# A fused attention and gated-MLP kernel: another order of all its steps, with two weight pieces decoded first and warm-up products on TensorE

## The chip, the cores and the metric

The kernel runs on one core of a Trainium2 chip. A core has four compute engines that the text calls PE (TensorE: matmuls, with PEld for its weight loads), DVE (VectorE), ACT (ScalarE) and POOL (GpSimd), and SP (SyncE), which here only issues DMA transfers. Each engine runs its own instructions strictly in order and waits at each for what it needs; sixteen DMA engines carry what SP issues. The metric is the device time of one execution in microseconds, as the median of several runs. One further execution was profiled, and all durations of single instructions come from it.

## The reference

For 4 batches, 8 heads, 768 tokens and head width 64, each chunk of 32 queries attends to 8 memory keys and to a window of keys from 16 before to 8 after the chunk. The result, as 768 tokens by 512 columns, goes through a gated MLP with a spatial product.

```python
for c in range(nc):                      # chunks of 32 tokens
    k_full = concat([mem_k, k[l_start:r_end]]); v_full = concat([mem_v, v[l_start:r_end]])
    scores = scale * q_c @ k_full.T
    a = exp(scores - max(scores)); a = a / (sum(a) + 1e-9)
    out[c] = a @ v_full
x = out                                   # (4, 768, 512)
h = gelu_tanh(x @ w_in)                   # (4, 768, 1024)
u, v = h[..., :512], h[..., 512:]
v_n = (v - mean(v)) / sqrt(var(v) + 1e-6) * g_ln
v_s = einsum('ts,bsd->btd', w_sg, v_n) + b_sg[None, :, None]
return x + (u * v_s) @ w_out
```

In this case the weights w_in and w_out arrive as 64-bit floating point numbers, seen by the kernel as two 32-bit words for each, so they must be decoded on the chip before they can be used.

## The kernel before

The work is cut into 24 attention units, one for each batch and each block of 128 tokens (unit u is batch u // 6, block u % 6), and into MLP products. Everything is written as named steps, and the string ORDER says in which order they are issued: each name is looked up and its instructions are appended to the program of its engine. Since every engine works in order, ORDER fixes the sequence on each engine, including SP's queue of transfers; across engines only data dependencies and the reuse of buffers hold work back. A star behind a name takes the step's second engine. Nothing else orders the work.

The steps, with the engine (second engine after a slash):

- `q`, `k`, `v` + u (SP): the transfers of a unit's queries (256 KB), keys (368 KB) and values (512 KB). There are two buffers for q and k and three for v, so q2 and k2 wait until unit 0's scores are done.
- `S` u (PE): scores; `mx` (DVE) row maxima; `sb` (DVE) subtraction, which also empties the single score buffer in PSUM, so that S of the next unit waits for it; `ex` (ACT) exponent; `z` (POOL) zeroes missing keys in the first and last block; `sm`, `sr` (DVE) sum and reciprocal; `nm` (DVE / POOL) normalising. `T` (PE) transposes the result and `p` (ACT / DVE) copies it to SBUF for units below 10; later units use `yt` (DVE) and the transfers `Ea` to `Ed`.
- `A` u (PE): the product with the values; `xc`, `xh` (ACT), `xl` (POOL / DVE, or DVE alone for units 0, 2, 4, 5): the result in 32 bits, and split into a high and a low part for the products that follow.
- `ri` + half + piece (SP): one of eight pieces of w_in, 512 KB each; half 1 is for v, half 0 for u. `d1` (ACT / POOL), `d2` (DVE / ACT), `d3`, `d4` (DVE), `d5` (ACT), `d6` (POOL / DVE) decode it into a high and a low part. Pieces i10 and i11 make up the first half of the columns for v, i12 and i13 the second. `ro` and `d..o` are the same for w_out; `g`, `ga`, `gb` load and split w_sg; `cb` and `cbh` the small vectors.
- `V` bt (PE): h for v, 12 products of 512 columns for a block of 128 tokens; `v1` to `v4` its gelu, `v5`, `vx`, `vy`, `v6` its statistics, `v7` normalising, `v8`, `v9` the split. `Va` and `Vb` are the two halves of V in 12 products of 256 columns each; blocks listed in VSPLIT are made that way.
- `U` bhj (PE): h for u, 12 products of 384 columns, `u1` to `u4` its gelu; `W` bhj (PE): the spatial product, 18 products; `w1` to `w4` gate it; `O` bhj (PE): the output product, 12 products; `o1` (DVE) adds x; `out` (SP) stores.
- `zz` + n: n warm-up products of the identity with itself, written into the PSUM buffer that is free next and read by nobody. Each is one 128-column product and appears in the trace as two matmul instructions.

T, V, U, W and O share four PSUM buffers, handed out in turn. Every operation is recorded through one helper, so the profile gives nearly all of them the line L106; they are told apart by their tiles: `s` scores, `e` exponents, `n` normalised, `av` the product with the values, `pt` its transposed factor, `raw`, `ex`, `m` the stages of decoding, `w_in_hi` and `w_in_lo` the decoded weights, `mm` the shared PSUM buffers, `pair` the split input.

```python
    def warm(n):
        for _ in range(n if mms.free else 0):
            tensor.matmul(mms.free[0][:, 0:P], ident, ident, start=True, stop=True)

    for name in ORDER.split():
        if name[0] == "z" and name[1] == "z":
            warm(int(name[2:]))
            continue
        does, eng = steps.pop(name.rstrip("*"))
        does(eng[name.endswith("*")])
```

Of the kernel before, what the change touches and what calls it, by code (L numbers as in the profile page):

```python
# [55 lines left out]
w4000 d6o2 w4002 w1012 S13 mx13 z12 sm12 w2012 A9 z11 sm11 w1011 w2011 w3012 sr11 nm11 yt11 O000 O003 sb13
o1003 O001 u2013 u3013 sr12 o1001 v12 k15 v10 S14 O002 mx14 W013 nm12 ex13 w3011 xh6 xh8 w4012 sb14 u4013 xh7
xl8 V12 w1013 w2013 v112 w3013 o1002 o1000 ex14 w4013* Ed5 Ea5 k16 q15 Ec5 q16 Eb5 out003 S15 out001 out002
out000 k17 w4011* xl7 sm14 v212 yt12 sr14 sm13 V11 v312 sr13 v111 v211 v311 w4010 xl6 O011 U101 nm13* mx15
v411 sb15 v412 v512 yt13 vx12 xc9 A10 u1101 xc10 S16 vy12 v612 v511 A11 ex15 sm15 o1011 vx11 vy11 v611 v711*  # L60
nm14* v712 v812 v912* V10 mx16 U103 v110 v210 v310 u1103 U102 sr15 u2101 v410 sb16 ex16 sm16 u3101 sr16 u4101
v510 u1102 O012 v811 vx10 o1012 q17 S17 mx17 k18 q18 Ea6 Ec6 Eb6 Ed6 out011 O013 O010 u2102 xc11 u3102 xh9
v911 vy10 v610 yt14 o1013 nm15 sb17 u2103 xl9* A12 S18 V13 yt15 v710* v810 xh10 xh11 u4102 xl11 o1010 u3103
v113 xl10 v213 v313 v413 v14 out012 v13 out010 out013 k19 q19 q20 k20 V15 U110 u1110 v513 vx13 u4103 v910 mx18
nm16 sb18 vy13 v613 v713* U113 V14 xc12 v115 v215 v315 u2110 v813 ex17 u1113 v913 A13 S19 v114 v415 v515 vx15
u2113 u3113 v214 v314 v414 v514 vx14 u4113 vy15 z17 v615 v715* U100 U112 U111 u1100 v815 ex18 vy14 v614 v714
u3110 v814 u4110 u1111 v914* u2100 u2111 u3111 u4111 v915 W111 w1111 w2111 sm17 Ed7 W103 w1103 w2103 mx19 W101
w1101 sr17 w3111 w4111 xc13 w3103 u3100 v15 Eb7 Ec7 v16 Ea7 yt16 nm17* W100 A14 w2101 sb19 S20 w3101 u1112
xc14 u2112 u3112 ex19 u4100 w1100 w2100 A15 W102 W110 w1102 w2102 W113 w1110 w1113 w3100 w3102 w2110 w2113
yt17 w4103 W112 w4100 w4102 z18 w4101 w1112 w3110 w3113 O100 w4110* O103 sm18 sr18 u4112 w2112 w3112 o1103  # L70
# [575 lines left out]
```

## Time and profile before

| | |
|---|---|
| median of 3 runs | 385.7 us (384.4 to 385.95) |
| profiled execution, its own time | 383.29 us |
| span of the profiled execution | 381.5 us |
| PE busy | 363.9 us, 95% of the span |
| DVE busy | 247.5 us, 65% |
| ACT busy | 155.3 us, 41% |
| POOL busy | 131.3 us, 34% |

The busy share is an average over stages that differ: the span begins with a stretch in which weights arrive and are decoded while the first units run, and goes on with a long stretch of MLP products. Time lost is read from the stretch where PE waits, by what ended its wait. The time of an execution is a little longer than the span from its first to its last instruction.

### The profile page before, as it was taken

The page shows a single profiled execution, that of the slowest core. Times are in us where ns is not written, and L with a number is a line of the kernel's source. Part 1 is how long each engine was busy: PE and PEld are TensorE (multiplying, and loading weights), DVE is VectorE, ACT ScalarE, POOL GpSimd, SP SyncE. Part 2 cuts the span into 40 slices and gives each one's busy share as a digit, 9 for nine tenths or more (in the row PEclk, how much of TensorE's full clock was granted, in tenths as well). Part 3 has the DMA queues.
Part 4 walks back from the last instruction along what each step waited for, and adds up shares of the span by engine and source line. Part 5 has one row for each costly group of instructions (what it writes and reads, how often), then busy time and mean ns, then how long its engine had stood idle before and what let it go on. Part 6 is the DMA issues. An engine that isn't in the chain of part 4 may idle for free.

```text
span 381.5 us, 11092 instructions
## 1 busy us (share of the span) xinstructions
PE 363.9 (95%) x4788; PEld 340.7 (89%) x4788; DVE 247.5 (65%) x460; ACT 155.3 (41%) x296; POOL 131.3 (34%) x152
## 2 busy tenths in 40 slices
...
GB/s 242 350 316 308 309 181 212 225 66 171 207 173 163 159 74 211 130 95 74 4 11 140 117 217 14 144 10 140 25 3 54 189 50 2 3 0 2 0 63 147
DMA packets 24530, 47.66 MB, mean 125 GB/s; under 512 B 4384, under 2 KB 13600, under 8 KB 24480
## 3 DMA queue, kind: packets, MB, share of 16 engines
...
HBM read 36.96 MB, written 6.29 MB: 113 GB/s over the span
## 4 chain that ended last, share of the span: by engine, by line
PE 94%; DMA 3%; issue 1%; DVE 1%; SPq 0%; POOL 0%; POOLq 0%
PE mmd L106 23%; PE mmc L106 22%; PE mmb L106 19%; PE mma L106 17%; PE av L106 7%; PE s L106 5%; DMA qb<-in_qs 2%; DMA ka<-in_ks 1%; SPq L106 0%; POOL na L106 0%; DVE ea L106 0%; DVE mxa L106 0%; DVE xb L106 0%; POOLq L106 0%
## 5 line engine op out<-in xcount | busy, mean ns | idle before, releaser
L106 PE MATMUL s<-ka,qa 64*32 64x64 f32 x768 | 11.0, 238 | 6.2 <-DMA ka<-in_ks 4.2
L106 PEld LDWEIGHTS s<-ka,qa 64*32 64x32 f32 x768 | 8.9, 112 | 7.9 <-issue 5.1
L106 DVE SCALAR_TENSOR_TENSOR mmc<-mmc,g_half,b_half 128x384 f32<-128x384 f32 x10 | 6.2, 623 | 12.4 <-PE mmc L106 12.4
L106 DVE SCALAR_TENSOR_TENSOR mmd<-mmd,g_half,b_half 128x384 f32<-128x384 f32 x12 | 7.4, 620 | 10.2 <-PE mmd L106 10.2
L106 DVE SCALAR_TENSOR_TENSOR gb<-gb,mmb 128x512 f32<-128x512 f32 x10 | 6.9, 686 | 9.3 <-ACT gb L106 9.3
L106 PE MATMUL s<-kb,qb 64*32 64x64 f32 x768 | 11.0, 238 | 1.7 <-DVE ea L106 1.5
L106 ACT ACTIVATE ea<-ea 128x512 f32<-128x512 f32 x12 | 7.6, 635 | 11.0 <-DVE ea L106 11.0
L106 DVE STREAM_TRANSPOSE y<-na 128x512 f32<-128x512 f32 x14 | 9.8, 702 | 3.4 <-POOL na L106 1.7
L106 PEld LDWEIGHTS s<-kb,qb 64*32 64x32 f32 x768 | 8.9, 112 | 3.5 <-DVE ea L106 1.8
L106 PEld LDWEIGHTS av<-pt,va 64*64 64x64 f32 x512 | 9.3, 145 | 2.9 <-ACT pt L106 1.7
L106 PE MATMUL av<-pt,va 64*64 64x32 f32 x512 | 10.2, 230 | 1.3 <-ACT pt L106 1.3
L106 PE MATMUL mmc<-w_in_hi,paira 128*128 128x512 f32 (+1 forms) x40 | 9.5, 359 | 1.8 <-issue 1.8
L106 DVE TENSOR_REDUCE mxa<-s 128x8 f32<-128x512 f32 x8 | 5.4, 679 | 8.5 <-PE s L106 8.5
L106 PEld LDWEIGHTS av<-pt,vb 64*64 64x64 f32 x512 | 9.2, 145 | 1.9 <-issue 1.1
L106 POOL TENSOR_TENSOR na<-eb,rda 128x512 f32<-128x512 f32 x3 | 3.5, 1169 | 20.2 <-DVE rda L106 16.4
L106 DVE SCALAR_TENSOR_TENSOR ga<-ga,mmb 128x512 f32<-128x512 f32 x6 | 4.1, 681 | 9.8 <-ACT ga L106 9.8
L106 POOL TENSOR_TENSOR pairb<-uf,pairb 128x384 fp32r<-128x384 f32 x3 | 3.0, 1016 | 20.9 <-ACT pairb L106 20.9
L106 PE MATMUL av<-pt,vb 64*64 64x32 f32 x512 | 10.2, 230 | 0.0
L106 DVE SCALAR_TENSOR_TENSOR mmb<-mmb,g_half,b_half 128x384 f32<-128x384 f32 x6 | 3.7, 617 | 9.9 <-PE mmb L106 9.9
L106 POOL TENSOR_TENSOR paira<-uc,paira 128x384 fp32r<-128x384 f32 x3 | 3.1, 1047 | 20.1 <-ACT paira L106 20.1
L106 ACT ACTIVATE ga<-ga 128x512 f32<-128x512 f32 x12 | 7.6, 632 | 6.0 <-DVE ga L106 5.9
L106 PEld LDWEIGHTS av<-pt,vc 64*64 64x64 f32 x512 | 8.4, 135 | 1.8 <-issue 1.3
...
## 6 DMA issues: line engine op xcount, KB each, us to landing
ka<-in_ks SPq DMA_DIRECT2D x12, 368.0 KB, 4.3
kb<-in_ks SPq DMA_DIRECT2D x12, 368.0 KB, 4.6
va<-in_vs SPq DMA_DIRECT2D x8, 512.0 KB, 5.4
vb<-in_vs SPq DMA_DIRECT2D x8, 512.0 KB, 4.8
vc<-in_vs SPq DMA_DIRECT2D x8, 512.0 KB, 4.6
pt<-y SPq DMA_DIRECT2D x112, 32.0 KB, 1.9
...
```

Of the source, the lines that this page charges most:

```text
L106: return self.tc.keep_in_program_order(getattr(self.engine, name)(*args, **kw))
```

## The change

The diff changes three things. VSPLIT shrinks to (0,), so V of blocks 1 and 2 of batch 0 is made in one piece. In `mm_part` the first half always takes a buffer. And ORDER is another string for all steps. Counted in the strings, the warm-up products go from 4 to 41: seventeen ahead of S0, seventeen between S0 and T0, five ahead of A2, and single ones ahead of A1 and V02. SP's queue now begins with ri11, ri10, k0, q0, ri13, ri12, q1, k1, v0, q2, k2, ri01, k3, q3, v1, ri00, k4, v2, q5, cb, q4, and the d steps of i11 and i10 stand ahead of mx0. PE's sequence begins: 17 products, S0, 17 products, T0, S1, A0, S2, Va00, Vb00, S3, T1, A1, T2, 5 products, A2, S4, T3, V01, S5, A3, V02, T4, S6, V03, U002, S7, A4, U001, U003, V04, T5, S8, A5, T6, U000, V05. Before it was: 3 products, S0, S1, S2, T0, A0, S3, T1, T2, A1, Va00, A2, Vb00, Va01, S4, Vb01, T3, Va02, A3, S5, Vb02, a product, S6, V03, U001, T4, U002, A4, S7, U003, V04, T5, S8, A5, T6, U000, V05. Beside the products, the set of steps is the same but for the halves of V01 and V02.

```diff
@@ -30,68 +30,68 @@
 DIRECT = (0, 2, 4, 5)
 N_U = 7
 ACTX = ()
-VSPLIT = (0,1,2,)
+VSPLIT = (0,)
 
 
 ORDER = """
-zz1 q1 q0 k0 k1 ri11 ri10 zz2 S0 mx0 sb0 ex0 z0 sm0 sr0 q2 k2 S1 mx1 sb1 S2 d2i11* d2i10* ex1 d3i11 d3i10 sm1
-d1i10 d4i10 sr1 v0 ri13 k3 q3 ri12 v1 nm0* d5i10 T0 p0 nm1* A0 mx2 sb2 ex2 sm2 d1i11 d2i13* d1i13 d4i11 d3i13
-sr2 d4i13 d6i10 S3 T1 nm2* T2 xh0 d5i11 xl0 d6i11 xc0 d5i13 p1* A1 d2i12* d1i12 mx3 sb3 d3i12 d6i13* d4i12 xc1
-ex3 sm3 p2 xh1 xl1* v2 d5i12 d6i12* q5 ri00 d2i00* d1i00 ri01 Va00 A2 Vb00 d2i01* d1i01 d3i00 d4i00 d3i01 sr3
-d4i01 d5i00 v100 xh2 v200 v300 q4 ri02 k4 xl2 cb ri03 v3 k5 Va01 S4 q6 k6 g21 g41 g20 g40 g11 nm3* Vb01 T3
-d5i01 d2i02* xc2 v101 p3 d2i03* d1i02 Va02 v400 v500 mx4 vx00 d3i02 cbh v201 sb4 vy00 v600 v700 v800 v900
-d3i03 d4i02 A3 S5 Vb02 mx5 sb5 zz1 S6 ex4 xc3 xh3 sm4 xl3 V03 v301 v401 sr4 v501 d1i03 v102 v202 d4i03 d5i03
-d5i02 v302 ex5 d6i00* nm4 d6i02* d6i01 q7 g10 v6 v4 k7 v5 U001 T4 vx01 vy01 z5 v601 d6i03* ga40 gb40 v402 mx6
-sm5 v701 sb6 u1001 ga11 p4 ga21 ga10 U002 v801 A4 S7 U003 v502 u1002 sr5 u2002 vx02 u2001 ex6 xh4 u3001 xl4
-v901* xc4 v103 u3002 ga41 gb21 gb11 nm5* vy02 z6 v602 gb10 v702* u4001 mx7 sm6 sb7 V04 g51 k8 q8 u4002 v203
-ex7 ga51 v303 T5 p5 sr6 nm6* v403 v503 S8 A5 T6 U000 ga20 v802 mx8 gb51 gb41 gb20 k9 ro0 g30 g01 ga01 xh5 v7
-q10 q9 g31 v902* vx03 gb01 p6 xl5 v104 u1003 xc5 vy03 v603 sb8 v204 u2003 sm7 sr7 u1000 u2000 nm7 V05 ex8
-u3003 ga31 v304 u4003 v703 v404 v803 S9 sm8 v504 vx04 sr8 mx9 v903 A6 T7 xc6 p7 v105 ga30 v205 u3000 g50 q11
-k10 v8 k11 ga50 v305 sb9 u4000 vy04 gb31 gb30 v405 v505 gb50* vx05 nm8* v604 U012 U011 g00 S10 k12 A7 u1012
-u2012 u3012 vy05 v605 mx10 v705 v704 T8 ex9 xc7 p8 U010 U013 v804 u4012 v904* v805 ga00 v905* sb10 A8 S11
-d2o0* d3o0 gb00 d1o0 u1010 ro1 sm9 u1011 d4o0 u2011 ex10 xc8 u2010 u3010 u4010 u3011 u4011 d1o1 W003 d2o1 mx11
...
+zz8 ri11 d1i11 d2i11 d3i11 d4i11 zz3 ri10 d2i10* d1i10 d3i10 d4i10 zz1 zz1 zz1 zz3 d5i11 d6i11 k0 q0 S0 zz4
+zz6 zz4 zz3 ri13 ri12 q1 k1 v0 q2 k2 ri01 d1i13 mx0 sb0 ex0 d2i13* z0 sm0 sr0 nm0 d2i12* d1i12 d3i13 d3i12
+d4i13 T0 S1 p0 A0 mx1 sb1 k3 q3 d5i10 d6i10 d5i13 d4i12 xh0 xl0 S2 Va00 d6i13 ex1 d5i12 d6i12 Vb00 mx2 sm1 sb2
+sr1 d2i01* ex2 d1i01 v100 xc0 S3 v1 ri00 k4 v2 d3i01 sm2 d4i01 mx3 sr2 nm1* T1 nm2* sb3 v200 zz1 p1 d2i00* ex3
+A1 T2 q5 cb q4 ri02 k5 v3 ri03 zz5 v300 xc1 p2 xh1 A2 S4 d3i00 sm3 sr3 nm3 v400 v500 xl1 T3 V01 d1i00 mx4 sb4
+vx00 d4i00 xh2 xl2 ex4 sm4 p3 d2i02* xc2 S5 A3 zz1 cbh vy00 v600 d3i02 sr4 v700 mx5 sb5 V02 nm4* k6 v5 q6 g10
+q7 g40 g11 v4 k7 g20 g21 g30 v101 d1i02 v800 d4i02 xc3 d2i03* d3i03 d5i00 d1i03 xh3 v201 d6i00* ex5 v301 xl3*
+d4i03 d5i02 v900* d5i01 d5i03 v102 T4 S6 d6i02* d6i03 v401 v501 v202 vx01 mx6 sb6 V03 U002 d6i01 z5 vy01 v601
+v701 ga10 p4 ga21 ga20 gb10* gb20* v801 u1002 v302 ga11 v901 gb21 gb11 S7 A4 sm5 sr5 v402 u2002 xh4 xl4 v502
+vx02 g50 k8 U001 ex6 u3002 u4002 z6 v103 u1001 ga40 u2001 v203 mx7 sm6 U003 V04 xc4 ga30 ga50 v303 v403 nm5*
+vy02 gb40 v602 sb7 sr6 q9 q8 g01 v6 k9 g41 ro0 v702 T5 S8 u3001 p5 A5 v802 ex7 u1003 ga41 nm6* u4001 v503 vx03
+mx8 T6 xh5 v902 vy03 v603 gb30 sb8 sm7 p6 v104 sr7 xl5 ex8 v204 sm8 v304 v703 v404 U000 u1000 xc5 nm7* v803
+v903 u2000 u2003 v504 vx04 V05 T7 S9 A6 p7 u3000 u4000 v105 v205 v305 xc6 d2o0* u3003 ga01 mx9 gb50 vy04 v604
+gb41* sr8 v704 sb9 nm8* v804 gb01* v904 v405 u4003 v505 q10 v8 k10 v7 k11 q11 g51 g00 U012 U011 A7 S10 ga51
+u1011 d1o0 d3o0 d4o0 mx10 u2011 vx05 T8 p8 vy05 v605 U013 U010 ga00 sb10 gb00* xc7 u3011 u4011 v705 v805 d5o0
+ex10 u1012 ex9 S11 A8 ro1 gb51* v905* W002 g31 q13 d2o1 u2012 u3012 d3o1 d1o1* d4o1 u4012 xc8 ga31 k12 ro2
...
@@ -482,7 +482,7 @@
 
         def mm_part(eng, h):
             hl = x_pair(b, tt // 3)
-            ps = mms.held[key] if key in mms.held else mms.take(key)
+            ps = mms.held[key] if h else mms.take(key)
             product(eng, ps[:, 256 * h:256 * h + 256], [
                 (lambda a, kt=kt: hl[:, a, kt, sl], lambda c, kt=kt: w_in_hl[c][:, 2 + h, kt])
                 for kt in range(4)
```

## Rows read from the trace of the kernel before

**Rows 1.** The page's first part: the span, and each engine's busy time with its share and its instructions.

```profile
span 381.5 us, 11092 instructions
...
PE 363.9 (95%) x4788; PEld 340.7 (89%) x4788; DVE 247.5 (65%) x460; ACT 155.3 (41%) x296; POOL 131.3 (34%) x152
```

**Rows 2.** Busy time by stretch: the stretch and its length, then for PE, PEld, DVE, ACT and POOL the busy us with the number of instructions, then the granted clock, the share of the DMA engines and what they moved in GB/s.

```profile
12.00:25.00 13.00, 9.09 (x268) 7.52 (x268) 11.99 (x21) 7.91 (x14) 5.54 (x5) 1.00 0.92 336
25.00:42.00 17.00, 15.17 (x346) 14.25 (x342) 14.92 (x27) 14.29 (x26) 8.88 (x8) 1.00 0.92 314
46.00:62.50 16.50, 16.50 (x329) 15.12 (x329) 13.73 (x27) 12.69 (x27) 14.04 (x17) 1.00 0.70 244
46.00:377.60 331.60, 331.60 (x3976) 312.47 (x3975) 214.19 (x402) 127.48 (x248) 115.67 (x129) 1.00 0.31 100
```

**Rows 3.** The chain that ended last in order of time: start, duration, what. The products of Va00, Vb00, the gap in Vb02, a warm-up product (two instructions), V03, T4, A4, S7, V05, O311, and the last addition.

```profile
25.27 2.86 PE mmd L106 x12
...
29.26 1.61 PE mmd L106 x12
...
39.51 1.83 issue
...
41.97 0.22 PE mmb L106 x2
...
42.98 3.00 PE mmb L106 x12
...
48.08 0.44 PE mma L106 x4
...
50.60 1.06 PE av L106 x64
51.66 0.79 PE s L106 x53
...
62.50 2.82 PE mmc L106 x12
...
375.55 2.10 PE mmb L106 x12
377.67 0.56 DVE xb L106
```

**Rows 4.** PE in order of time: start, duration, tile and shape, and in brackets the idle time before it and what ended that. The first warm-up products, S0, T1, T2, A1 and A2.

```profile
1.42 1.65 PE L106 MATMUL mma<-ident 128*128 128x128 f32 x6 [1.42 <-POOL mhalf L106]
7.28 1.17 PE L106 MATMUL s<-ka,qa 64*32 64x64 f32 x64 [4.21 <-DMA ka<-in_ks]
...
19.84 1.11 PE L106 MATMUL mmb<-ident,na 128*128 128x128 f32 x4
22.29 1.12 PE L106 MATMUL mmc<-ident,na 128*128 128x128 f32 x4 [1.33 <-POOL na L106]
23.33 1.93 PE L106 MATMUL av<-pt,vb 64*64 64x32 f32 x64
...
28.05 1.20 PE L106 MATMUL av<-pt,vc 64*64 64x32 f32 x64
```

**Rows 5.** DVE in order of time, same columns: mx0, sb0, sm0, sr0, d3 of i11 and of i10, and xl5.

```profile
8.49 0.69 DVE L106 TENSOR_REDUCE mxa<-s 128x8 f32<-128x512 f32 x1 [8.49 <-PE s L106]
9.21 0.69 DVE L106 TENSOR_TENSOR ea<-s,mxa 128x512 f32<-128x512 f32 x1
10.85 0.69 DVE L106 TENSOR_REDUCE rda<-ea 128x8 f32<-128x520 f32 x1 [0.95 <-POOL ea L106]
11.58 0.20 DVE L106 RECIPROCAL rda<-rda 128x8 f32<-128x8 f32 x1
...
12.98 0.68 DVE L106 SCALAR_TENSOR_TENSOR exb<-rawb,exb 128x512 int32<-128x512 int32 x1
13.58 0.69 DVE L106 SCALAR_TENSOR_TENSOR exa<-rawa,exa 128x512 int32<-128x512 int32 x1
...
61.46 0.69 DVE L106 TENSOR_TENSOR pairb<-av,pairb 128x512 fp32r<-128x512 f32 x1 [0.75 <-ACT pairb L106]
```

**Rows 6.** ACT and POOL in order of time, same columns: ex0, two steps of decoding back to back on ACT; on POOL z0, nm0 and a lower part of decoded weights.

```profile
9.94 0.63 ACT L106 ACTIVATE ea<-ea 128x512 f32<-128x512 f32 x1 [7.93 <-DVE ea L106]
...
10.62 0.20 POOL L106 MEMSET ea<- 32x128 f32 x1 [9.21 <-ACT ea L106]
...
11.94 1.04 POOL L106 TENSOR_TENSOR na<-ea,rda 128x512 f32<-128x512 f32 x1 [1.12 <-DVE rda L106]
...
22.19 1.28 POOL L106 TENSOR_TENSOR w_in_lo<-mb,w_in_hi 128x512 fp32r<-128x512 f32 x1
...
29.00 0.68 ACT L106 ACTIVATE exf<-rawf 128x512 int32<-128x512 uint32 x1
...
29.56 0.69 ACT L106 ACTIVATE mf<-rawf 128x512 f32<-128x512 f32 x1
```

**Rows 7.** Transfers: what had moved in the first 7.2 and the first 8.1 us, and single issues with size and us from issue to landing: k3 (issued at 11.17) and v1 (12.71).

```profile
DMA packets 688, 1.71 MB, mean 238 GB/s; under 512 B 72, under 2 KB 72, under 8 KB 688
...
DMA packets 783, 2.08 MB, mean 256 GB/s; under 512 B 76, under 2 KB 76, under 8 KB 783
...
kb<-in_ks SPq DMA_DIRECT2D x1, 368.0 KB, 6.8
...
vb<-in_vs SPq DMA_DIRECT2D x1, 512.0 KB, 8.4
```

More of the change, by code (lines that the diff above doesn't have):

```diff
@@ L56 @@
[L56 to L70, printed above, removed]
@@ new lines @@
+W001 mx11 w1002 w2002 sm9 sr9 nm9* gb31* d2o2* d6o0* w1001 w2001 w3001 u1010 d1o2 sb11 d3o2 u2010 u3010 W003
+w1003 w2003 W000 u4010 d4o2 T9 w1000 d5o2 ex11 v9 q12 ro3 S12 k13 q14 d6o2 w4001 sm10 p9* w2000 d1o3 w3003
+d5o1 w3000 W010 sr10 w1010 w2010 mx12 w4003 u1013 w3010 w3002 W012 W011 w4000* d6o1 z11 sm11 nm10 d2o3* d3o3
+d4o3 d5o3 sb12 ex12 z12 yt10 d6o3* w4002* S13 mx13 sr11 nm11* w4010 w1012 sm12 w2012 A9 O003 O002 o1003 u2013
+sb13 w1011 w2011 sr12 yt11 O000 O001 xh8 xl8 o1000 o1001 xh6 k14 v10 q15 k15 v11 S14 W013 u3013 mx14 u4013 xh7
@@ new lines @@
+ex13 o1002 w1013 w2013 sm13 xl6 nm12* sb14 V12 w3012 xl7* w4012 Ec5 out003 Ea5 q16 Ed5 out001 k16 out002 S15
+Eb5 out000 v12 U101 V11 v112 v212 w3013 sr13 ex14 w3011 u1101 u2101 w4011* w4013 O011 xc9 A10 v111 v312 yt12
+mx15 nm13 v211 sb15 v412 yt13 sm14 v512 xc10 vx12 S16 u3101 v311 A11 xc11 vy12 v612 v712 v812 ex15 V10 v411
+mx16 o1011 v511 sr14 v912 v110 vx11 v210 v310 v410 v510 u4101 nm14* sb16 vx10 sm15 vy11 v611 v711* U102 v811
+v911* vy10 O010 O012 O013 sr15 o1012 o1013 xh10 xl10* k17 q17 Eb6 Ec6 Ed6 Ea6 U103 A12 S17 xh9 xh11 u1102 xl11
@@ new lines @@
+v610 xl9* yt14 o1010 V13 ex16 u1103 sm16 nm15* mx17 sr16 u2102 sb17 ex17 u3102 u2103 yt15 v710* v810 u4102
+v113 v213 u3103 v313 v413 v910 z17 nm16* v13 out013 out012 v15 k18 k19 q18 out010 v14 out011 q19 V15 v115 v215
+v513 vx13 v315 xc12 v415 v515 u4103 vy13 v613 v713 v813 v913 vx15 U110 u1110 u2110 sm17 V14 U113 S18 U100 v114
+v214 v314 vy15 v615 mx18 sb18 u3110 u1113 v414 v514 vx14 u2113 A13 S19 u1100 v715* v815 v915 u3113 u2100 u3100
+vy14 v614 u4100 u4110 u4113 v714 U112 u1112 v814 v914* sr17 U111 W103 u2112 w1103 w2103 W113 W101 Eb7 k20 Ec7
@@ new lines @@
+yt18 xl14 o1113 sr19 V21 v420 o1110 v520 xl15 V23 A16 nm19* vx20 vy20 v620 v720 o1111 yt19 v820 v920 v121 xc16
+v221 v321 v421 v521 vx21 S21 A17 U202 V22 xh16 v123 mx21 v223 u1202 vy21 v621 v721 v821 v323 xc17 v921 v423
+v523 u2202 v122 xh17 xl16* vx23 vy23 v623 u3202 v222 u4202 xl17 U201 u1201 u2201 u3201 v322 v422 v522 sm20
+U203 u1203 u2203 vx22 v723 v823 q22 out113 out111 v19 Ed9 out110 Ec9 v18 Eb9 q23 Ea9 k23 sr20 u4201 U200 V24
+sb21 v923* u1200 V25 v124 ex21 vy22 v622 u3203 nm20 v722 v822 v224 v324 u2200 u4203 v424 v922* S22 A18 mx22
@@ new lines @@
+v125 v225 xc18 v325 u3200 sb22 v425 sm21 v525 U210 U211 U212 u1210 v524 sr21 vx24 u4200 u2210 vy24 v624 v724
+vx25 vy25 v625 u3210 v725 u4210 u1212 ex22 v824 v825 U213 v925* A19 S23 mx23 u2212 u3212 u4212 v924 W200 W211
+sm22 sr22 yt20 w1200 nm21* w2200 w3200 u1211 u2211 u3211 sb23 xc19 w1211 u4211 w4200 w2211 u1213 w3211 ex23
+W203 w1203 w2203 yt21 W201 w3203 w4203* W210 w1210 w2210 w1201 w2201 w3201 u2213 u3213 Ed10 v20 Eb10 Ec10 v21
+Ea10 u4213 W202 w1202 w2202 w4201 w3210 z23 nm22 yt22 w3202 w4211 w4202 W213 w1213 W212 w1212 w2212 w3212
@@ new lines @@
+w4210* sm23 A20 O201 o1201 w2213 w3213 w4213* w4212* xc20 O203 o1203 sr23 nm23 yt23 O200 A21 O202 O211 O212
+xh19 xh20 o1202 xl20* o1200 o1212 Eb11 out202 Ea11 v22 out203 out212 Ec11 out200 V32 v132 v232 out201 v23 xl19
+V31 v131 o1211 out211 Ed11 v332 v432 v231 xh18 v331 v431 xl18 O213 O210 U301 xc21 xh21 v532 vx32 vy32 v632
+o1213 v732 xl21* A22 U302 v832 u1301 xc22 xh22 v932* v531 u2301 vx31 vy31 v631 u3301 u1302 u2302 u4301 V30
+v130 v230 v330 U303 A23 xl22* v731* v430 u1303 u2303 v530 o1210 V34 vx30 u3302 u4302 xc23 u3303 v831 v931*
```

39 lines of the change are left out of this document (12 added, 27 removed).

## The prediction

> **What bounds the kernel now.** I began with the page's busy line: PE works 95% of the span [rows 1]. The table by stretch says where the other 5% lies [rows 2]: from 46 to 377.6 us PE is busy in all 331.6 us, at 12 to 25 us in 9.1 of 13, at 25 to 42 in 15.2 of 17. The chain of waits in order of time [rows 3] repeats it: from V03's first product (42.98) piece follows piece without a gap until O311 ends at 377.65, and 3.85 us of addition and store close the span. So what comes before 46 us, the ramp, is the one place where time can be won, and a new wait after it the likeliest way to lose some.
>
> In the ramp two things are slow. First, PE runs at its lower level: the twelve products of Va00 took 2.86 us, the same twelve of Vb00 1.61 [rows 3]; a set of transposes 1.11 us at 19.84, 0.44 at 48.08 [rows 3, 4]. [...] Second, DVE: 12.0 of 13 us at 12 to 25, 14.9 of 17 at 25 to 42, 13.7 of 16.5 at 46 to 62.5 [rows 2]. PE waits for it; after 46 us it has a sixth of its time free.
>
> **The change part by part: how early V03 can end.** V03's last product ends at 45.98 in the kernel before [rows 3]. I walk the new order to the same point. Prices: a DVE operation of 512 columns takes 0.69 us but the next starts 0.60 after it when ready (12.98, 13.58), and 0.72 when it needs the result (8.49, 9.21) [rows 5]; ACT starts one each 0.56 (29.00, 29.56); POOL takes 1.28 for a lower part [rows 6]; PE at the upper level 0.79 for scores, 0.44 for transposes, 1.06 for A, 2.8 for V (3.00 right behind scores), 0.22 for a warm-up product [rows 3]; at the lower level three such products took 1.65, or 0.55 each [rows 4].
>
> *Seventeen products ahead of S0.* From 1.42 us they end at 5.2 if all cost 0.22, at 10.8 if all cost 0.55. I take the middle, 8.0.
>
> *S0's data.* ri11 and ri10 (512 KB each) now precede k0 and q0 (368 and 256 KB): 1.69 MB in that order. Before, 1.71 MB had moved by 7.2 us and 2.08 MB by 8.1 [rows 7], so in strict order S0 could start near 7.2. But k0, third of six transfers then, was there only at 7.28 [rows 4], when 1.71 MB had moved instead of the 0.90 MB up to it: later transfers share the engines. Five more follow at once now, so the end could be near 10. I take 8.4. [...] By strict order S0 would come 1.2 us sooner; the trace's 7.28 stands against counting on it.
>
> *Two pieces decoded in DVE's idle time.* Five DVE operations (d2 to d4 of i11, d3 and d4 of i10, 5 × 0.60 = 3.0 us) move to before mx0; until 8.49 DVE had nothing to do [rows 5]. If ri10 lands only near 7 they end near 8.5, before S0 does. That is the gain's source on DVE. ACT's d1, d2 and d5 hide the same way; if this cover were gone, 3.0 us of DVE would be back on the ramp.
>
> *Unit 0.* S0 ends at 9.2. The chain mx0 to sr0 took 8.49 to 11.78 before [rows 5]; nm0, now on DVE (0.69 against POOL's 1.04 [rows 6]), ends near 13.2. PE meanwhile does the second seventeen products: 3.7 us at the upper level, done at 12.95, so T0 starts at 13.25. A0 follows its copy at 14.5 to 15.6, S1 sits between. d3 and d4 of i13 and d3 of i12, mx1, sb1, d4i12 fill DVE up to 16.8; xl0 waits for xh0 and ends at 17.5. Va00 starts there, against 25.27 [rows 3]. i12's lower part on POOL ends at 18.9, Vb00 at 20.5.
>
> *From Vb00 to V03.* PE has left S3, S4, S5, S6 (4 × 0.79), T1 to T4 (4 × 0.44), A1 to A3 (3 × 1.06), three V (8.4), seven products (1.5) and 0.6 for changes of kind: 18.6 us, so 39.1 with no wait. Waits I see: A1 for v1, which is issued only near 15.4 because k3 and q3 stand ahead of it and wait for S1; such a transfer took 8.4 us [rows 7], so A1 starts near 23.9; then V01 for xl1 on POOL (28.0). Together about 1.8 us: V03 ends at 40.9. Merging Va/Vb of units 1 and 2 costs nothing on PE (24 short products of 1.40 us per half against 12 long of 2.8), and gives up only a start on half the weights that nobody needs once all four pieces are decoded.
>
> That is 45.98 − 40.9 = 5.1 us sooner, and T4 (0.44) is already done, where before it came after: 5.5.
>
> *What is given back.* Counting DVE operations in the order (full 0.605, 384-column 0.47, tiny 0.12), those up to xl5 come to 44.1 us before and 45.0 after, of which 3.0 now lie ahead of mx0: 42.0 from about 9.2, so 51 with no idle. Before, the same stretch held 9.6 us of idle (8.49 to 62.15 [rows 5]). The new V05 could start near 57.3 for PE (16.3 us behind V03, as 45.98 to 62.50 [rows 3]). With 6 us of idle DVE keeps up; with all 9.6 V05 starts near 60.7 and only 2 us are left. I charge 1.0 between these. Later stages hold the same products, and PE's order within them is alike; the close of 3.85 us too. Sum: 5.5 − 1.0 = 4.5 us.
>
> **The rivals.**
> *The ramp stays DVE- or transfer-bound:* DVE idles as before, or the 8.6 MB up to q4, at the 336 GB/s of 12 to 25 us [rows 2], arrive at 27.4 and each later unit slips. For it: DVE's and the transfers' shares there. Against it: much of DVE's idle time came after PE had become the bound. Gain 0 to 2: 384.7.
> *The clock stays low and the products stand in the way:* the second seventeen then cost 0.55 each, 9.35 us, and T0, A0 and all that DVE does for unit 0 queue behind them. With the first seventeen ending at 10.8 and S0, at 1.17, at 12.0, T0 starts at 21.3 instead of 13.25; 8 us later, less 4.5: 3.5 slower, 389.2. It decides when more than about half of them are at the low price. [...]
> *New waits after 46 us:* there are none before, but the new order sets T5, A5 and T6 right behind their producers (nm5, p5, nm6), and W002 behind v905. Each could cost 0.5 to 1; over 4.5 in sum makes it slower, 386 to 388. Against it: the old order has as many places with no distance (V05 directly behind xl5) and lost nothing.
> *PE never waits in the ramp:* V03 at 39 and the 1.83 us gap of Vb02 [rows 3], which no engine explains, gone: gain 7 to 8, 378.
>
> **How the numbers follow.** The profiled execution took 383.29 us around a span of 381.5; 4.5 less is 378.8. The runs' median is 385.7, 2.4 above it, so the forecast is 381.2. Half a percent (1.9 us) is about what this kernel's runs can tell from nothing. Chances: forecast (gain 2 to 6.5) 0.60, larger gain 0.06, slow ramp 0.18, low clock 0.07, later waits 0.09. The forecast's own range is 379.2 to 383.7; with the slow ramp and part of the later waits 378.5 to 386.5, which leaves out some 0.17. Faster by over 0.5%: 0.60 + 0.06 + a little of the slow ramp = 0.68; slower: 0.12; the rest 0.20.
>
> **What would show it.** S0 at 8 to 9 us in 0.8 instead of 1.17; T0 at 13 to 14; Va00's first product near 17.5; V03's end at 40 to 42; PE full from there; DVE busy before 8.5. The prediction is wrong if T0 starts after 16, if scores still take 1.17 beyond 9 us, or if PE has gaps behind V03 worth more than 2 us.

## The result, and the profile after

| | after | before |
|---|---|---|
| median of 6 runs each | 388.65 us (387.01 to 390.18) | 384.14 us (383.03 to 385.95) |
| ratio, 95% interval | 1.0107 (1.0068 to 1.0147) | |
| profiled execution, its own time | 390.05 us | 383.29 us |
| span | 388.2 us | 381.5 us |

The change made the kernel slower by 4.5 us; forecast were 4.5 us the other way. Medians are of all executions; ratios leave out those more than 1.5% above the fastest of their kernel. The two profiled executions lie further apart than the medians, by 6.8 us, and the sums below are about these two. The page of the changed kernel, its busy line and the line of one DMA queue (packets, MB, share of the 16 engines):

```profile
span 388.2 us, 11193 instructions
PE 373.5 (96%) x4838; PEld 349.3 (90%) x4838; DVE 251.0 (65%) x468; ACT 153.7 (40%) x295; POOL 118.1 (30%) x145
q8 instruction: 38, 0.62, 0.7%
```

PE is busy 9.6 us longer than in [rows 1]; the groups of warm-up products ahead of S0 and ahead of T0 alone take 6.93 and 4.06 us (below). The table by stretch (columns as in [rows 2]):

```profile
12.00:25.00 13.00, 10.17 (x355) 8.93 (x353) 12.74 (x24) 9.48 (x17) 6.57 (x5) 1.00 0.89 315
25.00:42.00 17.00, 13.56 (x303) 11.30 (x304) 8.54 (x17) 8.03 (x15) 5.93 (x6) 0.80 0.72 256
46.00:384.70 338.70, 335.18 (x3981) 315.48 (x3979) 220.13 (x416) 126.43 (x248) 103.12 (x123) 0.99 0.32 100
...
31.40:38.20 6.80, 6.03 (x44) 4.80 (x41) 4.41 (x9) 2.15 (x4) 3.06 (x4) 0.50 0.75 269
232.80:236.10 3.30, 3.30 (x11) 3.19 (x10) 0.00 (x0) 0.54 (x2) 0.00 (x0) 0.50 0.13 32
...
127.00:140.00 13.00, 11.44 (x234) 10.02 (x233) 9.99 (x20) 5.37 (x10) 3.58 (x6) 1.00 0.43 131
224.00:240.00 16.00, 14.11 (x238) 12.37 (x237) 8.92 (x18) 6.48 (x13) 4.80 (x8) 0.89 0.26 76
```

At 12 to 25 us PE does more than before. At 25 to 42 it does less (13.56 against 15.17), DVE is busy in only half of the stretch (8.54; before 14.92), and the granted clock is 0.80: half speed from 31.4 to 38.2. Behind 46 us PE, which never paused before, now idles 3.5 us, and it has a second stretch at half speed. PE in order of time, with the idle time before a group and what ended it in brackets:

```profile
1.42 6.93 PE L106 MATMUL mma<-ident 128*128 128x128 f32 x34 [1.42 <-POOL mhalf L106]
8.28 0.86 PE L106 MATMUL s<-ka,qa 64*32 64x64 f32 x64
9.07 4.06 PE L106 MATMUL mma<-ident 128*128 128x128 f32 x34
13.26 0.66 PE L106 MATMUL mma<-ident,na 128*128 128x128 f32 x4
...
22.72 1.01 PE L106 MATMUL av<-pt,vb 64*64 64x32 f32 x54 [0.45 <-ACT pt L106]
26.03 0.41 PE L106 MATMUL av<-pt,vb 64*64 64x32 f32 x10 [2.30 <-issue]
...
30.86 0.63 PE L106 MATMUL s<-ka,qa 64*32 64x64 f32 x39 [1.64 <-DMA qa<-in_qs]
32.26 0.65 PE L106 MATMUL s<-ka,qa 64*32 64x64 f32 x25 [0.77 <-issue]
```

and the chain that ended last (start, duration, what):

```profile
17.61 3.06 PE mmb L106 x24
20.67 0.80 PE s L106 x53
...
22.88 7.84 DMA qa<-in_qs
...
32.91 1.04 PE mma L106 x4
33.95 4.78 PE mmc L106 x12
...
45.02 3.00 PE mma L106 x12
48.01 2.10 PE mmc L106 x12
...
132.82 0.82 PE av L106 x46
133.64 1.56 issue
...
228.79 0.69 PE av L106 x35
229.48 1.89 issue
231.37 0.66 PE av L106 x29
232.03 3.50 PE mmc L106 x12
235.53 3.14 PE mmb L106 x12
...
384.67 0.56 DVE xb L106
```

Up to Vb00 (end 20.67) PE went as forecast. Then A1 stops after 54 of its 64 products for 2.30 us, S4 waits for q4 and then stops after 39 for 0.77, T3 and V01 run at half speed (1.04 and 4.78), and V03 ends at 48.01, where before it ended at 45.98 [rows 3]. A11 and A17 stop in the same way in their middle, for 1.56 and 1.89, and U202 and V22 behind A17, 232 to 239 us, run partly at half speed.

The sum: the last addition starts at 384.67, before at 377.67 [rows 3], 7.0 later. V03 ends 2.03 later, less T4 that is already done (0.44), 1.6; the two late stops 3.45; U202 and V22 (3.50 + 3.14, against 2.28 and 2.79 for such pieces at full clock) 1.57. That is 6.6; the last 0.4 I did not find.

**What the four stops have in common.** "Issue" means that no engine and no transfer shown ended the wait. So I counted. Each product in PE's rows has its weight load, and each of the two is one instruction, so that a warm-up product (two rows) counts four. The trace has 99 more of PE's sequencer (96 semaphore events and 3 drains), which PE's rows above do not show and which count as well. Taken in order of start, the stops lie behind 961, 1217, 4801 and 7105 instructions, and the 1.83 us of the kernel before [rows 3] behind 1473. All are 193 and a multiple of 256. The queue q8, named instruction, moves 38 packets of 16,384 bytes, one for 256 of PE's 9,775 instructions (9,676 products and loads, and those 99), at 64 bytes each. The first packet is taken for the block that begins behind instruction 449, the next packet for the next block, and so on. The trace's records then give (us; "instruction" is the number of instructions ahead of the stop, "entered" the start of the block before, "last start" and "next start" are those of the instructions on either side of the boundary):

```
kernel  instruction  block before entered  packet         last start before  next start
before     1473            36.57           39.05-40.02         39.23           41.34
after       961            20.04           23.58-24.54         23.51           26.03
after      1217            26.03           29.85-30.86         31.27           32.25
after      4801           131.55          132.62-133.84       133.42          135.21
after      7105           227.37          228.53-229.87       229.26          231.37
```

PE resumes 1.3 to 1.5 us behind the packet's end. S and A units hold 128 instructions each and take about 0.8 and 1.06 us, a V or U unit 24 in 2 to 2.8 us. So where a block falls together with a run of S and A units (A10 S16 A11, A16 S21 A17), its 256 instructions are gone in 1.9 us, before the next packet has come. That is the theory; its rivals are the order (a late q4, cb, a wait of some step that the profile doesn't name) and the clock. The clock did not make the stop at 133.4: it stood at 1.00 from 127 to 140 us. Of the theory the trace shows the queue, the size and count of its packets (q8, 16,384 bytes, 38) and the times in the five rows.

### The profile page after: what moved, and what is told of

Same layout as the page of the kernel before. It is cut to its first block, busy times and chain, and to the rows that moved or that the text cites. A ratio compares the mean times of both kernels' runs of the same rounds, so it can differ in the third digit from the quotient of the medians.

```text
span 388.2 us, 11193 instructions
## 1 busy us (share of the span) xinstructions
PE 373.5 (96%) x4838; PEld 349.3 (90%) x4838; DVE 251.0 (65%) x468; ACT 153.7 (40%) x295; POOL 118.1 (30%) x145
## 4 chain that ended last, share of the span: by engine, by line
PE 93%; DMA 2%; DVE 2%; issue 1%; SPq 0%; POOL 0%; ACT 0%; DVEq 0%; POOLq 0%
PE mma L106 21%; PE mmb L106 21%; PE mmc L106 21%; PE mmd L106 19%; PE av L106 6%; PE s L106 5%; DMA qa<-in_qs 2%; SPq L106 0%; DVE rda L106 0%; DVE ea L106 0%; DVE mxa L106 0%; DVE eb L106 0%; DVE exd L106 0%; ACT ea L106 0%; DVE paira L106 0%
## 5 line engine op out<-in xcount | busy, mean ns | idle before, releaser
L106 PE MATMUL mma<-ident 128*128 128x128 f32 x78 | 12.3, 330 | 1.4 <-POOL mhalf L106 1.4
L106 PEld LDWEIGHTS mma<-ident 128*128 128x128 f32 x78 | 11.8, 243 | 1.5 <-POOL mhalf L106 1.4
L106 PE MATMUL av<-pt,vc 64*64 64x32 f32 x512 | 9.7, 221 | 3.5 <-issue 3.5
L106 PE MATMUL mmc<-paira,w_in_hi 128*128 128x384 f32 x56 | 12.1, 363 | 0.0
L106 PE MATMUL mma<-w_in_hi,pairb 128*128 128x512 f32 x40 | 11.0, 397 | 0.0
L106 PEld LDWEIGHTS mmc<-paira,w_in_hi 128*128 128x128 f32 x56 | 10.8, 206 | 0.0
L106 PE MATMUL mma<-pairb,w_out_hi 128*128 128x384 f32 x56 | 10.8, 336 | 0.0
L106 DVE SCALAR_TENSOR_TENSOR mma<-mma,g_half,b_half 128x384 f32<-128x384 f32 x7 | 4.3, 617 | 9.2 <-PE mma L106 9.2
L106 PE MATMUL mmc<-w_in_hi,paira 128*128 128x512 f32 x32 | 10.3, 448 | 0.0
L106 PEld LDWEIGHTS mma<-pairb,w_out_hi 128*128 128x128 f32 x56 | 9.8, 188 | 0.0
```

Source lines behind the costliest of these rows:

```text
L106: return self.tc.keep_in_program_order(getattr(self.engine, name)(*args, **kw))
```

## The experiments

Times are medians; ratios go to the kernel before, timed along with each. The diffs show the steps of ORDER that move.

**e1: is it q4 behind cb?** Bias and gain (cb, cbh) go later, q4 moves up.

```diff
-T2 q5 cb q4 ri02 k5 v3 ri03 zz5 ... zz1 cbh vy00 ... v601 v701
+T2 q5 q4 ri02 k5 v3 ri03 cb zz5 ... zz1 vy00 ... v601 cbh v701
```

> The changed kernel with the two small vectors' transfers (cb) moved behind ri03, so that q4 no longer stands behind them, and their halving (cbh) moved back accordingly. Theory 1 (q4 is late because it queues behind cb): S4 starts near 28 us instead of 30.9, PE's clock does not fall to 0.5 in the 30 to 38 us stretch, V01 takes 2.8 to 3.0 us instead of 4.8, V03 ends near 43 to 44 instead of 48.0, and the time falls by about 4 us, to 384 to 385. Rival (the 16 DMA engines are simply full there, the order within the queue does not matter): q4 lands within 1 us of before, time unchanged within 1 us of 388.6.

Measured 387.94 us, ratio 1.0076 (1.0034 to 1.0118). PE in order of time:

```profile
25.36 0.41 PE L107 MATMUL av<-pt,vb 64*64 64x32 f32 x10 [1.75 <-issue]
31.64 0.65 PE L107 MATMUL s<-ka,qa 64*32 64x64 f32 x25 [0.89 <-issue]
```

S4 no longer waits for q4, but the stops stay at the same instructions, after 54 and 39 products, and so does the low clock (V01 4.50 us). V03 ends at 47.13, 0.9 us earlier, and even this may be the difference between two executions: e2 below has the changed kernel's ramp step for step, and there V03 ends at 47.31. The time did not fall by the 4 us of theory 1; the late q4 was not the main cause.

**e2: are the late stops the dense runs?** A11 and A17 each move behind a V or U unit.

```diff
-A10 ... S16 ... A11 xc11 ... V10 ...      A16 ... S21 A17 U202
+A10 ... S16 ... V10 A11 xc11 ...          A16 ... S21 U202 A17
```

> The changed kernel with two triples of small products broken up on PE: A10 S16 A11 becomes A10 S16 V10 A11, and A16 S21 A17 becomes A16 S21 U202 A17. Theory 2 (PE outruns the fetch of its own instructions, 256 at a time, where three units of small products stand together and a whole block is used up in under 2 us): the gaps of 1.6 us in A11 and 1.9 us in A17 vanish, with them the fall of the clock behind the second, and the time falls by 3 to 5 us to 384 to 385.5. Rival (the gaps are waits for the exchanged blocks Ea to Ed, or chance): the gaps stay inside A11 and A17, time unchanged within 1 us.

Measured 385.14 us, ratio 1.001 (0.997 to 1.005): 3.5 us of the loss are back. The same two stretches as above, by the same columns:

```profile
127.00:140.00 13.00, 13.00 (x244) 11.58 (x243) 10.79 (x21) 6.06 (x11) 4.95 (x7) 1.00 0.34 110
224.00:240.00 16.00, 16.00 (x261) 14.46 (x260) 11.82 (x23) 8.86 (x17) 5.44 (x8) 1.00 0.39 117
```

PE is busy throughout and the clock stands at 1.00. The ramp was left alone: its stops (2.03 and 1.44) stand at the same instructions, but in this execution S4 does not wait for q4, and V03 ends at 47.31, 0.7 us sooner than in the changed kernel's.

**e3: both edits together.**

> Both edits. If theories 1 and 2 both hold and their costs are at different places, the gains add: 8 us less than the changed kernel, 380 to 381.5, which is 3 us under the kernel before. If either falls, only the other's gain is seen.

Measured 384.07 us, ratio 0.9989 (0.9953 to 1.0025), not the 380 to 381.5 of two gains added. The ramp still has stops of 1.94 and 0.60 at the same instructions, V01 4.76, V03 at 48.40.

**e4: only the gain (cg, 2 KB in pieces of 4 bytes) behind ri03, the bias stays with cb (the halving, cbh, moves back as in e1).**

```diff
-        eng.dma_start(g_half, g_ln.rearrange("(k p) -> p k", p=P))
         eng.dma_start(b_half, b_sg.partition_broadcast(P))
+    def load_g(eng):
+        eng.dma_start(g_half, g_ln.rearrange("(k p) -> p k", p=P))
```

> The changed kernel with cb left where it is, but only for the 384 KB vector; the 2 KB vector, 512 single numbers of 4 bytes, is loaded behind ri03. If the many tiny pieces are what slows the DMA engines at 24 to 28 us, this brings nearly all of what moving both brings: 4 us. If the 384 KB ahead of q4 are what counts (about 1 us at 400 GB/s), it brings under 1 us.

Measured 387.5 us, ratio 1.0036 (1.0 to 1.0073). q4 lands at 28.62 instead of 30.72, yet S4's stop grows to 1.59: what q4 gives, the block takes. V03 ends at 46.80, the late stops stay.

**e5, e6, e7: fewer products, the order kept.** If blocks are counted, taking products away must move the stops, though the units around them are untouched. e5 keeps the first 17 only, e6 the 4 of the kernel before, e7 the first 34.

```diff
 e5:  -S0 zz4 zz6 zz4 zz3 ... zz1 p1 ... zz5 v300 ... A3 zz1
      +S0 ... p1 ... v300 ... A3
 e7:  -zz1 p1 ... zz5 v300 ... A3 zz1
      +p1 ... v300 ... A3
```

> The changed kernel with only the seventeen products ahead of S0; the 24 behind S0 (96 of PE's instructions in the trace) are left out, both triples of small products stay. Theory 2 in its strict form (a gap falls where PE's count of instructions passes a multiple of 256 and the block before was used up in under 3 us): the two later boundaries move 96 instructions on, out of the reach that makes a whole block fast, so the gaps in A11 and A17 vanish although A10 S16 A11 and A16 S21 A17 stand as they were: 3 us less. In the ramp the gap moves from A1 into A2. If the products keep the clock up, T0 and S1 now run at the lower level (1.1 and 1.17 us). Rival (the triples make the gap wherever the count stands): gaps of 1.5 to 2 us stay.

> The changed order with the four products of the kernel before in the kernel before's places, 37 fewer than the changed kernel. Rival on the products (they only use up instructions, of which the ramp can fetch 256 in 5 to 6 us): 148 fewer bring V03's end about 3 us sooner, 45 us, and with the later gaps gone the time is 382 to 383. Theory of the change (they keep PE at the upper level, which the early half V needs): without them S0 to Vb00 run at the lower level, Va00 takes 2.9 us, V03 ends 2 us later, 50 us, and only the later gaps are gained, 386 to 387.

> The changed kernel without the seven products that stand ahead of A1, A2 and V02; the 34 around S0 stay. Strict theory 2: the boundaries move 28 instructions on, so the later gaps stay but sit elsewhere: in A17 after about 49 of its 64 matmuls instead of 35, in A11 after about 60 instead of 46 and shorter. The ramp has 28 fewer instructions to fetch, 0.6 us; the time is 387 to 388. Rival (gaps tied to the place in the program, such as the transfers they wait for): still after 35 and 46.

Measured: e5 386.19 us, 1.0035 (1.0001 to 1.007), profiled at 389.47 us, the longest of its ten; e6 386.03, 1.0046 (1.0021 to 1.007); e7 387.58, 1.009 (1.0053 to 1.0126). In e5 and e6 both late stops are gone with the runs A10 S16 A11 and A16 S21 A17 in place. In e7 they stay, but 28 instructions of products fewer put A11's behind 60 products instead of 46 (0.68 us) and A17's behind 49 instead of 35 (1.28). 28 instructions are 14 of A's with their loads: both moved by exactly that. The order alone is out as a cause, the count is in. Where a stop comes is not told by the count alone, though: e5's boundary in A2 passed without the stop that was expected there. New stops come in other places (e7 and e5, PE in order of time):

```profile
32.60 0.46 PE L106 MATMUL s<-ka,qa 64*32 64x64 f32 x13 [2.75 <-issue]
135.01 0.30 PE L106 MATMUL av<-pt,vc 64*64 64x32 f32 x4 [0.68 <-issue]
```

```profile
41.32 1.20 PE L106 MATMUL mmd<-w_in_lo,paira 128*128 128x512 f32 x4 [0.84 <-issue]
62.28 0.43 PE L106 MATMUL av<-pt,vc 64*64 64x32 f32 x15 [1.40 <-issue]
```

They also show what the products bring. In e6 S0 takes 1.17 us and Vb00 ends at 23.38, 2.7 later than with the 41; its V03 ends at 46.53 (45 or 50 expected), 1.5 earlier than with the 41.

**e8: the kernel before with 17 products at its start** (14 more, 56 instructions, while PE has nothing else to do).

```diff
-zz1 q1 q0 ... ri11 ri10 zz2 S0
+zz8 q1 q0 ... ri11 ri10 zz9 S0
```

> The kernel before with seventeen products at the start instead of three, in the time in which PE waits for k0. If the clock alone held back its ramp: S0, S1, S2, T0 and A0 run at the upper level, but DVE and the transfers still set the pace up to 25 us; Va00 still starts after 23 us and the time falls by 1 us at most. If it costs instructions to fetch: 56 more move the gap in Vb02 back to the middle of S5 and the time rises by 0 to 1.5 us.

Measured 386.3 us, ratio 1.0059 (1.003 to 1.0088). PE in order of time:

```profile
21.47 0.44 PE L106 MATMUL s<-kb,qb 64*32 64x64 f32 x9 [1.74 <-issue]
...
42.11 0.41 PE L106 MATMUL s<-kb,qb 64*32 64x64 f32 x20 [1.09 <-issue]
```

Fourteen more products, made while PE had nothing else to do, made the kernel slower: S3 now stops for 1.74, and Va00 still takes 2.86.

**e9 to e12: which ramp is best?** All have e2's two moves. e9 to e11 put q4 ahead of k4 and cb behind ri03; e9 has 4 products, e10 all 41. e11 has 4 and 4 products of 512 columns in place of the 41 of 128, 32 instructions for 164. e12 is e11 with the transfers in the changed order.

```diff
-            tensor.matmul(mms.free[0][:, 0:P], ident, ident, start=True, stop=True)
+            tensor.matmul(
+                mms.free[0].rearrange("p (a c) -> p a c", a=4), ident,
+                ident.unsqueeze(1).broadcast_to([P, 4, P]), start=True, stop=True,
+            )
```

> The changed order with both triples broken up, the four products of the kernel before in place of the 41, cb behind ri03, and q4 issued ahead of k4 instead of behind q5 and cb. In the run without the products S4 waited until 31.5 us for q4; here q4 is issued near 18 and is there by 25. Theory 3 (in the ramp either q4 or the fetch of instructions is what PE waits for, and either alone hides the other): S4 near 28, V01 at the upper level, V03 ends at 43 to 44, no gap over 1 us later; 382 to 383.5. Rival (another limit, DVE or the clock, stands right behind): V03 still ends after 46, 385 to 386.

> The same with all 41 products. Theory 3 with a price on instructions: q4 is early, but the blocks of 256 that hold S3 to S4 still take 5.5 to 6.5 us each, so gaps of 2 and 1 us in A1 and S4 stay and V03 ends at 46 to 47.5: 384 to 385.5, 1.5 to 3 us over the run without products. If products cost nothing but PE time: level with it or faster by the clock, 381 to 383.

> The same with eight warm-up products of 512 columns, four ahead of S0 and four ahead of T0, in place of the 41 of 128: about the same time on PE in the two groups, 32 instructions instead of 164. If the products' instructions are their price and the clock their gain, this has both: V00 done by 21 as in the changed kernel, no gap over 1 us in A1 and S4, V03 ends at 42 to 43.5, 380 to 382, under the kernel before. Rival: as in the run without products.

> The changed kernel with both triples broken up and the eight wide products, its transfers in its own order. Against the run with the triples alone broken up it tells what the products' instructions cost: with theory 3 the gap in A1 shrinks below 1 us, then S4 waits for q4 instead, to 29 to 31 us; 383 to 385. If q4 did not matter it comes level with the run that also has q4 early.

Measured: e9 384.06 us, 1.0004 (0.9963 to 1.0045); e10 386.11, 1.0053 (1.0019 to 1.0087); e11 386.23, 1.0017 (0.9984 to 1.005); e12 388.96, 1.0123 (1.0052 to 1.0193). All four lie above what was expected. e10 has stops of 2.86 in A1 and 1.56 in S4; e12 waits for q4 until 31 us and stops for 2.91 ahead of T6. e12 differs from e2 in its warm-up products alone and is slower, where e2 was level with the kernel before: fewer instructions did not pay there. e11 comes nearest to the ramp that I had forecast, with V03's end at 40.9 (its chain, and a stretch by the columns of [rows 2]):

```profile
39.88 2.98 PE mma L106 x12
42.86 2.09 PE mmc L106 x12
...
56.74 2.56 issue
...
59.78 3.84 PE mmb L106 x12
63.62 3.49 PE mma L106 x12
```

```profile
58.20:65.00 6.80, 5.70 (x17) 5.41 (x18) 3.71 (x8) 3.52 (x7) 1.54 (x2) 0.50 0.56 203
```

V03 ends at 42.86, 3.1 us before [rows 3]. Then T6 stops for 2.56 us: S8 and A5 fill a block, which takes 2.11. Behind it the clock is at half for 6.8 us, and U000 and V05 take 3.84 and 3.49. With 1.75 us of waits at 127 to 156 us, that is all of the lead and more.

**e13, e14: is the stop ahead of T6 the block or the place?** e13 moves U003 and V04 between S8 and A5; e14 keeps e11's order and has 17 products of 128 columns at the start instead of 4 of 512, 52 instructions more.

```diff
 e13: -U003 V04 xc4 ... T5 S8 u3001 p5 A5
      +xc4 ... T5 S8 U003 V04 u3001 p5 A5
```

> The kernel of e11 (q4 ahead of k4, the bias and gain behind ri03, A11 and A17 moved, 4 and 4 warm-up products of 512 columns) with U003 and V04 moved from ahead of T5 to between S8 and A5. In e11 the 256 TensorE instructions from the start of S8 to T6 were S8 and A5 alone and took 2.11 us, their successors came 2.56 us late, and the clock fell after it (U000 3.84 us instead of about 2.1). With the move the same 256 instructions are the last 80 of S8, U003, V04 and A5: by durations of e11 0.5 + 2.3 + 2.8 + 1.1 = 6.7 us, longer than the 4.9 us from the start of that block to the start of the next. Theory of the instruction blocks: no gap between 54 and 62 us, no low clock there, U000 at 2.1 to 2.3 us, all of e11's 2.56 + 1.7 + some 0.8 us given back less the 0.6 us waits that it still has: 381 us +/- 1, ratio to the kernel before 0.988 to 0.995. Theory that the gap belongs to the place (T6 waits for the tile na or for PSUM): a gap of 2 us or more ahead of T6 stays, 385 to 387 us. Theory that the lead of the ramp is always eaten by the softmax behind it (DVE, ACT): no gap named issue, but TensorE waits for pt or xa ahead of A5 to A7, 384 to 386 us.

> The kernel of e11 with the first group of warm-up products as 17 of 128 columns (68 instructions) in place of 4 of 512 (16): the order of all steps, T5 S8 A5 T6 too, is e11's, and every later block boundary falls 52 instructions earlier. Theory of the instruction blocks: the boundary that lay in T6 falls at some 38 of 64 matmuls of A5, and the block ahead of it now has some 52 instructions of U003 and V04 (about 5 us at 0.1 us each) ahead of S8: no gap at T6; the gaps of the ramp change their places (the one in S2 after 9 of 64 goes ahead of it, into A0 or the first of S2). If the ramp is no worse, 381 to 384 us. Theory that the gap belongs to the place: the 2.56 us ahead of T6 stay, 386 us.

Measured: e13 391.24 us, 1.0157 (1.012 to 1.0193); e14 390.1, 1.0119 (1.0079 to 1.016). Both were expected at 381 to 384. Neither has the stop; e14's T6, in the old order, follows A5 without a gap:

```profile
63.98 1.13 PE L106 MATMUL av<-pt,vc 64*64 64x32 f32 x64
65.05 0.66 PE L106 MATMUL mma<-ident,na 128*128 128x128 f32 x4
```

So it was the block. But both lost elsewhere: e14 stops three times in its ramp (2.42, 1.75, 2.27), and V03 ends at 51.72; in e13 T5 and S8, now ahead of U003 and V04, come before their inputs and wait 2.74 for POOL and 1.74 for DVE.

**e15, e16: ten products, the same edit in two kernels.** Forty instructions right behind V03, in e11 and in the kernel before.

```diff
-V03 U002            (e11)        -V03 v301    (before)
+V03 zz10 U002                    +V03 zz10 v301
```

> The kernel of e11 with ten warm-up products of 128 columns (40 instructions, some 0.6 us) added right behind V03, the order of all steps else as in e11. Theory of the instruction blocks, worked out by shifting e11's own start times: every boundary behind V03 falls 40 instructions earlier, so the block that took 2.11 us ahead of T6 becomes one that takes 4.8 us and ends some 56 of 64 matmuls into A5 (needed in e11: 4.9): gap there 0 to 0.5 us, no low clock behind it; the other short blocks are 4.0 us at 169 us (as in e11, no gap there) and 3.5 us at 261 us (gap 0 to 0.7). So e11's 2.56 + 1.7 + 0.7 us go, 0.6 come: 382 us +/- 1, ratio to the kernel before 0.990 to 0.998. Theory that products only cost and that the gap belongs to the place or to the softmax: e11's time plus 0.6 us, 387 us.

> The kernel before with the same ten products (40 instructions, some 0.6 us) right behind its V03 and nothing else. Theory of the instruction blocks, by the start times of the kernel before: the boundary behind V03 moves ahead of A4, so A4 and S7 lie in one block of 2.3 us: gap of 2 to 2.9 us at 52 us, in the unit behind S7; further short blocks of 3.2 us at 82 us (gap 0.2 to 1), 2.2 us at 149 us (gap 1.2 to 2) and 3.5 us at 255 us (gap 0 to 0.7); the gap of 1.83 us at 39.5 stays. Sum with the products: 4 to 7 us slower, more by 1 to 2 us for each fall of the clock: 388 to 392 us, ratio 1.010 to 1.020. Theory that products cost their own time only: 385 us, ratio 1.001 to 1.002.

Measured: e15 385.8 us (12 runs, 383.82 to 390.09), ratio 1.0025 (1.0003 to 1.0047); e16 386.91 us (12 runs, 383.75 to 391.37), ratio 1.0041 (1.0002 to 1.008). Neither number came. In e15 the stop moved from T6 into A5, behind 47 of its 64 products (some 56 expected), and shrank from 2.56 to 1.16 (0 to 0.5 expected), but two others appeared, and the profiled execution took 390.09 us, the longest of the twelve. In e16's profiled execution (386.27 us) the block with A4 and S7 took 2.25 us and had no stop at all:

```
kernel  instruction  block before entered  packet         last start before  next start
e11        2241            54.36           56.78-57.70         56.47           59.30
e14        2241            58.84           58.47-59.43         64.56           64.57
e15        2241            56.22           60.05-61.09         60.99           62.37
e11         705            17.46           20.29-21.31         22.93           22.93
e15         705            17.41           22.62-23.60         22.90           24.96
before     1985            50.78           50.62-51.51         55.51           55.51
e16        1985            53.20           49.99-51.01         55.46           55.46
```

Two things of my sum were too simple. A packet need not wait until its forerunner block is entered: in e16 it moved 3.2 us ahead of that, while slow U products stood in front of the boundary, so that the block's own length mattered little. And its start varies: e11, e13 and e15 are the same program up to V03, yet the packet for 705 started 2.8, 3.2 and 5.2 us behind the entry; the last, in that longest execution, cost 1.85 us. The changed kernel and e2 are the same up to A11, and there the packet for 705 started 0.67 and 2.42 us behind the entry.

**All traces together.** The 18 traces of this study have 661 block boundaries. In 52 the next instruction came over 0.5 us behind its forerunner, in every one of them 1.23 to 1.60 us behind the end of the packet; at no boundary did it come sooner than 1.23 behind it. The stops over 0.5 us that the profile puts down to "issue" on PE are all among these. Up to 62 us a packet started 2.4 us behind the entry of the block before (median of 137), later 0.65 us (of 524). What sets a packet's start was not tested: that the data transfers of the ramp delay it fits these two numbers and is not shown by them.

## Why the prediction was wrong

*Up to Vb00 it was right.* S0 started at 8.28 (8.4 forecast), T0 at 13.26 (13.25), Va00 at 17.61 (17.5), Vb00 ended at 20.67 (20.5). The first seventeen ended at 8.35, near the middle value of 8.0; the second took 4.06, near the 3.7 of the higher level. DVE decoded in its idle time as said.

*The step that failed is "From Vb00 to V03".* It set 18.6 us of products and 1.8 of waits; it took 27.34. Found are the two stops, 3.07; q4, 1.64; the low clock, 0.60 in T3 and 2.0 in V01; A1's wait for its pt, 0.45. That leaves about 1 us of small change. The waits that I had listed there, v1 and xl1, did not come. PE's instructions were costed by their durations alone, a product at 0.22 us, a score unit at 0.79. That these short ones also use up the stream of instructions, 128 for each S or A, was no term of the sum. S3, T1 and A1 follow each other without a V between them, and a block ended in A1; another ended in S4. In e11, which between Vb00 and V03 has neither a stop nor a late q4, the same way takes 20.33 us (22.53 to 42.86), near the 20.4 that I had set; it has seven products fewer, though (1.5 us), and waits 1.5 for pt in place of v1 and xl1, so that the match is part luck.

*A second step failed with it:* "Later stages hold the same products, and PE's order within them is alike", which left the stages behind V03 at nothing beside the 1.0 for DVE. The runs showed 3.45 us of stops in A11 and A17 and 1.57 of low clock there, and in e2, without them, 3.5 us of the loss are gone. My own sign of being wrong, gaps of more than 2 us behind V03, came true.

*q4 was read in a rival only.* The sum followed ri11 to v1 through SP's queue; q4 stands in the rival of the transfers alone, at 27.4 by its place in the bytes. But the new order sets it behind q5, which waits for S3, and behind cb's two transfers: it was issued at 22.88, took 7.84 and landed at 30.72. e1 shows that this was not decisive: without it the stops remain.

*The rivals.* "The ramp stays DVE- or transfer-bound" came true for the 1.64 us of q4 and not for DVE, which was busy for 8.54 of the 17 us at 25 to 42. "PE never waits in the ramp" named the right row, the 1.83 us "which no engine explains", and drew the wrong thing from it: I let it vanish with the order, where it was the first sign of what was to come. "New waits after 46 us" had the sign and, at 3.45 us and 1.57 of clock, the size, but its places were wrong: T5, A5, T6 and W002 waited for none of their producers.

"The clock stays low" did not happen: S0 took 0.86 behind the seventeen products (1.17 behind three, in [rows 4] and in e6), and the granted clock stood at 1.00 from 7.5 us on. That the products would raise it was an estimate of mine. It fell to 0.50 at 31.4 us, behind A1's stop (2.30) and the wait for q4 (1.64). Other falls came behind idle time of PE too. Behind the 2.56 us stop of e11 and the 1.89 us stop at 229 us the granted clock stood at 0.50 (58.2 to 65.0 and 232.8 to 236.1 us); without the late stops there was no such fall behind A17, in e2 (1.00 at 224 to 240 us) and also in e5 and e6 (U202 and V22 took 2.29 and 2.78 us, and 2.28 and 2.78, against 3.50 and 3.14), where the runs of small products stay in place. In the ramp e1 and e6 part the two kinds of idle time. In e1 A1's stop (1.75) remains and S4 does not wait for q4; e6's ramp has no stop, and S4 waits 2.32 for q4. The clock falls in both (e1's stretch, e6's S4, e6's stretch; columns as above):

```profile
26.70:37.00 10.30, 9.41 (x150) 7.86 (x149) 6.16 (x12) 4.12 (x8) 2.85 (x4) 0.50 0.85 291
...
31.47 0.85 PE L106 MATMUL s<-ka,qa 64*32 64x64 f32 x64 [2.32 <-DMA qa<-in_qs]
...
32.20:35.60 3.40, 3.40 (x21) 2.87 (x11) 3.21 (x7) 1.74 (x4) 1.61 (x3) 0.50 1.02 410
```

Not every stop brought a fall: none came behind the 1.83 us of the kernel before (1.00 over 25 to 42 us [rows 2], then V03 in 3.00), the 1.56 in A11 (1.00 at 127 to 140 us) or the 1.28 in e7's A17 (U202 and V22 2.29 and 2.78 us). Which idle time does is open.

*What was given back* (1.0 us for DVE) was never tried: PE came late, and DVE idled half of 25 to 42 us. Two readings near it were loose, without weight in the sum: DVE has a sixth of its time free at 46 to 62.5 us and about a third in all that follows V03 [rows 2], and V05 lay 16.5 us behind V03 before, not 16.3.

*Does a faster ramp pay at all?* Open. e11 had it, 3.1 us, and lost it to one stop and its clock; no version here kept it, and none beat the kernel before by what can be measured (e3 0.9989, e9 1.0004, both with the interval across 1). The kernel before has one stop, of 1.83 us; its other boundaries lie in places that passed without.
